# Routing keys fetched back from DRAM one batch at a time, and the last two slots' gating on VectorE

## The chip, the cores and the metric

The kernel runs on one core of a Trainium2 chip. The metric is the device time of one execution in microseconds. The engines are TensorE (PE; PEld is its loading of weights), VectorE (DVE), ScalarE (ACT), GpSimd (POOL) and SyncE (SP), which here only issues DMAs. All of them run their own instructions in program order, so an instruction that waits holds everything behind it on its engine.

## The reference

Three layers, each fed by the one before: an attention with a memory (batch 4, 8 heads, 576 positions, 64 wide), a mixture of 8 experts in which each expert takes exactly 288 of the 2304 tokens, and a dense layer with a gated activation.

```python
logits = x @ w_gate                       # 2304 tokens x 8 experts
order = np.argsort(-logits.flatten())
for idx in order:                         # greedy: best pair first
    tok, e = (int(idx) // E, int(idx) % E)
    if assigned[tok] >= 0 or counts[e] >= cap:   # cap = 288
        continue
    assigned[tok] = e
    counts[e] += 1
...
h = np.maximum(x[mask] @ w1[e], 0.0)      # 512 -> 1024, per expert
out[mask] = h @ w2[e]                     # 1024 -> 512
...
h = x @ w_in                              # 512 -> 2048, all tokens
g = h * np.clip(h + 3.0, 0.0, 6.0) / 6.0
return g @ w_out                          # 2048 -> 512
```

## The kernel before

After attention (the first 270 us or so) the function `experts` works through 8 slots, one expert's 288 tokens each. A slot has two stages. Stage 1 is the expert's layer: 8 chunks of 128 hidden units (`order` with kind 0). Stage 2 is the dense layer on the same tokens: 16 chunks (kind 1). A chunk is a first product `l1` into a PSUM tile h (L1240, L1241, L1243), its activation on other engines (`ev`, L1249 on), and two chunks later (`LAG`) a second product `l2` that adds into four PSUM tiles acc (`mm3`, L1136 to L1138). From slot 1 on every factor is split into a high and a low part in a reduced fp32 format, so each chunk costs 24 matmuls of 288 columns.

Stage 1's activation is two ScalarE operations for t and gh, and VectorE's gl = t − gh (L1254). Stage 2's is t and pc on ScalarE (L1258, L1259), a second pass for t (L1260), the product t * pc on GpSimd (L1261), gh on ScalarE (L1262) and gl = t − gh on GpSimd (L1263). At the end of stage 1 `y_in` empties acc into yh (ScalarE) and yl (VectorE, L1210), the input of stage 2; at the end of stage 2 `out_units` empties acc into yo (half of them on VectorE, L1178), which are transposed and scattered to the output rows.

Weights: stage 1's come in as raw and are split by ScalarE and GpSimd (L1127, L1128). Of stage 2's, the odd chunks stay in SBUF (WB), the even ones are fetched already split, 512 KB a time, by SP (w<-hl, L1124) when one of a few buffers comes free.

The greedy assignment is done by the class `Router`, in phases, one per expert. Each phase takes the best open expert of each token (`best`), puts the key of each (token, expert) pair on rows (`turn`), spreads them over 128 partitions, and searches for the threshold that leaves 288 (`search`: compare all 2304 keys at L715, count, refine; four steps on the high halves rHw, then on the low halves rLw). `ids_units` then counts positions (roc at L946, the counting matmuls rp at L702) and makes the row lists (ids, L959). Phases from 2 on spread the keys through DRAM: `by_dram` writes them to kd (64 rows, L761) and reads each half back with each expert's row repeated on 16 partitions, 128 x 2304 of 16 bits, 576 KB (L765). Attention ends with one such call too.

A phase runs while an earlier slot computes: it is a generator, and `step`, called twice per chunk, takes as many of its pieces as the numbers that it yields allow (BACK = 6 after rHw's issue, SLACK = 2.3 per search step; RATE per call of `step`). So the pieces land between the chunks in program order; the tile framework then orders the instructions of each engine by its own estimate of when they can start. In the profiled execution the slots lie at 468 to 555 us (slot 1), 555 to 644, 644 to 738 (slot 3), 738 to 837 (slot 4), 837 to 924, 924 to 1006 and 1006 to 1087 (slot 7). The searches run in slots up to 4; slots 5 to 7 have none, and slots 6 and 7 have no routing.

Of the kernel before, what the change touches and what calls it, by code (L numbers as in the profile page):

```python
# [9 lines left out]
F32 = mybir.dt.float32  # L10
# [4 lines left out]
AF = mybir.ActivationFunctionType  # L15
OP = mybir.AluOpType
# [10 lines left out]
BACK = 6  # L27
# [487 lines left out]
class Router:  # L515
# [233 lines left out]
    def by_dram(self, wait=False):  # L749


        nc, ps, E, B, S = self.nc, self.ps, self.E, self.B, self.S
        n = 2 * E * B
        ks = self.wk.tile([n, S], U16, name="ks", bufs=1)
        kd = self.dram.tile([2, E, B, S], U16, name="kd", bufs=2)
        for i in range(2):
            c = slice(i * S // 2, (i + 1) * S // 2)
            p = ps.tile([128, 512], F32, name="rw", tag=self.tags[0], bufs=self.tags[1])
            self.mm(p[:n, :S // 2], self.RB.rearrange("p d e b -> p (d e b)"), self.XT[:, c], start=True, stop=True)
            nc.scalar.activation(ks[:, c], p[:n, :S // 2], AF.Copy)  # L760
        nc.sync.dma_start(kd.rearrange("d e b s -> (d e b) s"), ks)  # L761

        def back(d, W):
            src = kd[d].rearrange("e b s -> e (b s)")
            nc.sync.dma_start(W.rearrange("p b s -> p (b s)"), bass.AP(  # L765
                tensor=src.tensor, offset=src.offset, ap=[[B * S, E], [0, 128 // E], [1, B * S]]))
        back(0, self.Hw)
        low = lambda: back(1, self.Lw)
        if wait:
            return low  # L770
        low()

    def early(self, ps, *tags):

# [38 lines left out]
    def phase(self, s):  # L813
# [6 lines left out]
        if s < E - 1:  # L820
            if s:
                with self.later(s):
                    self.best(slice(0, B))
                yield 1 if s == 1 else 3
            self.turn(s <= 1)
            yield 1
            if s == 0:
                self.last_batch()
            elif s < DIRECT:
                yield from self.direct()  # L830
            else:
                low = self.by_dram(True)
                yield BACK
            half = SHARE if s <= 1 else 0
            Hs = self.search(self.Hw, cap - half, self.rowH, 2 * half)
            next(Hs)
            yield next(Hs)
            if s >= DIRECT:
                low()
            for y in Hs:  # L840
                yield y
            Bv = self.found
            nc.vector.tensor_scalar(self.cmp, self.Hw, Bv, None, op0=OP.is_equal)
            yield 1
            nc.vector.tensor_tensor(self.Lw, self.Lw, self.cmp, op=OP.mult)
            Ls = self.search(self.Lw, self.rem, self.rowL, 2 * half)
            next(Ls)

            m = wk.tile([128, 4, 32], F32, name="m", bufs=1)
            c = self.rowH[:, :, :32]  # L850
            if half:
                nc.vector.tensor_scalar(m, c, float(half), None, op0=OP.add)
                c = m
            nc.vector.scalar_tensor_tensor(m, c, cap, c, op0=OP.is_lt, op1=OP.mult)
            nc.vector.tensor_tensor(m, m, self.own[:, None, :].to_broadcast([128, 4, 32]), op=OP.mult)
            cnt = wk.tile([128, 1], F32, name="cnt", bufs=2)
            nc.vector.tensor_reduce(cnt, m, axis=AX.XY, op=OP.max)
            nc.vector.tensor_scalar(self.rem, cnt, -1.0, cap - half, op0=OP.mult, op1=OP.add)
            rhs = wk.tile([128, 2, E], F32, name="rhs", bufs=1)
            nc.vector.tensor_scalar(rhs[:, 0, :], self.sel, Bv, None, op0=OP.mult)  # L860
            yield 2
            for y in Ls:
                yield y
            nc.vector.tensor_scalar(rhs[:, 1, :], self.sel, self.found, None, op0=OP.mult)
            yield 2
            if s == 0:
                yield None
            ps = self.ps
            p = ps.tile([128, 512], F32, name="rp", tag="r", bufs=2)
            self.mm(p[:, :2 * E], self.onef, rhs.rearrange("p a e -> p (a e)"), start=True, stop=True)  # L870
            hl = wk.tile([128, 2, E], I32, name="hl", bufs=1)
            nc.vector.tensor_scalar(hl[:, 0, :], p[:, :E], 128.0, None, op0=OP.max)
            nc.vector.tensor_copy(hl[:, 1, :], p[:, E:2 * E])
            k = wk.tile([128, E], I32, name="k", bufs=1)
            th = wk.tile([128, E], I32, name="th", bufs=1)
            nc.vector.scalar_tensor_tensor(k, hl[:, 0, :], 16, hl[:, 1, :], op0=OP.logical_shift_left,
                                           op1=OP.bitwise_or)
            nc.vector.tensor_scalar(th, k, 31, -1, op0=OP.arith_shift_right, op1=OP.bitwise_xor)
            nc.vector.scalar_tensor_tensor(th, th, -2 ** 31, k, op0=OP.bitwise_or, op1=OP.bitwise_xor)
            thf = th.bitcast(F32)  # L880
            top = wk.tile([128, 1], F32, name="top", bufs=1)
            u = wk.tile([128, E], F32, name="u", bufs=1)
            nc.vector.tensor_reduce(top, thf, axis=AX.X, op=OP.max)
            nc.vector.scalar_tensor_tensor(u, thf, top, self.w8, op0=OP.is_equal, op1=OP.mult)
            nc.vector.tensor_reduce(code, u, axis=AX.X, op=OP.max)
            oe = wk.tile([128, NJ], F32, name="oe", bufs=1)
            nc.vector.tensor_scalar(oe, m2, code, None, op0=OP.is_equal)
            nc.vector.scalar_tensor_tensor(GQ[:, 0, :], mx, top, oe, op0=OP.is_gt, op1=OP.mult)
            nc.vector.scalar_tensor_tensor(GQ[:, 1, :], mx, top, oe, op0=OP.is_equal, op1=OP.mult)
        else:  # L890
            nc.vector.tensor_copy(code, self.left)
            nc.vector.tensor_scalar(GQ[:, 0, :], dead, 0.0, None, op0=OP.is_equal)
            nc.vector.memset(GQ[:, 1, :], 0.0)
# [132 lines left out]
def experts(ctx, tc, rt, x_dram, cv, w1, w2, out, ident, cap, B, S):  # L1026
# [184 lines left out]
            y.append(hl)  # L1211
        return y

    def l1_whole(kind, f, x, w, prev=None):
        p = ps.tile([128, 512], F32, name="h", tag="h", bufs=2)[:, :cap]
        for k in range(KC):
            rt.behind = nc.tensor.matmul(p, w[:, k * 128:(k + 1) * 128], x[k], start=(k == 0), stop=(k == KC - 1))  # L1217
            if prev is not None:
                after(tc, rt.behind, prev)
                prev = None  # L1220

        def ev():
            g = whole("g", "g", LAG + 2)
            if kind == 0:
                nc.scalar.activation(g, p, AF.Relu)
            else:
                t = act.tile([128, cap], F32, name="t", tag="t", bufs=2)
                pc = act.tile([128, cap], F32, name="pc", tag="pc", bufs=2)
                nc.scalar.activation(t, p, AF.Relu, bias=rt.three)
                nc.scalar.activation(pc, p, AF.Copy, scale=1.0 / 6.0)  # L1230
                nc.vector.scalar_tensor_tensor(g, t, 6.0, pc, op0=OP.min, op1=OP.mult)
            return g
        return ev

    def l1(kind, f, x, w, prev=None):
        hi, lo = w
        p = ps.tile([128, 512], F32, name="h", tag="h", bufs=2)[:, :cap]
        wk = [[z[:, k * 128:(k + 1) * 128] for z in (hi, lo)] for k in range(KC)]
# [9 lines left out]
        def ev():  # L1248
            gh, gl = parts("g", "g", LAG + 2)  # L1249
            t = act.tile([128, cap], F32, name="t", tag="t", bufs=2)  # L1250
            if kind == 0:
                nc.scalar.activation(t, p, AF.Relu)
                nc.scalar.activation(gh, p, AF.Relu)  # L1253
                nc.vector.tensor_tensor(gl, t, gh.bitcast(F32), op=OP.subtract)  # L1254
            else:

                pc = act.tile([128, cap], F32, name="pc", tag="pc", bufs=2)
                nc.scalar.activation(t, p, AF.Relu, bias=rt.three, scale=-1.0)  # L1258
                nc.scalar.activation(pc, p, AF.Copy, scale=1.0 / 6.0)  # L1259
                nc.scalar.activation(t, t, AF.Relu, bias=rt.six, scale=-1.0)  # L1260
                nc.gpsimd.tensor_tensor(t, t, pc, op=OP.mult)  # L1261
                nc.scalar.activation(gh, t, AF.Copy)  # L1262
                nc.gpsimd.tensor_tensor(gl, t, gh.bitcast(F32), op=OP.subtract)  # L1263
            return gh, gl
        return ev

# [53 lines left out]
    for i, (s, kind, f) in enumerate(order):  # L1320
# [14 lines left out]
        ahead(i)  # L1335
        for u in range(min(2 if kind else 1, len(conv)) if i else 0):
            conv.pop(0)()
        e = (l1 if s else l1_whole)(kind, f, X[s, 1] if kind else XT[s], W.pop((i, 0)) if s else raws[i][0],
                                    rt.behind if kind and f == 1 else None)
        step()  # L1340
        if len(pend) == LAG:
# [88 lines left out]
```

## Time and profile before

| | us |
|---|---|
| runs of the kernel before: 1089.23, 1094.15, 1103.21; median | 1094.15 |
| the profiled execution | 1098.72 |
| its span, first to last instruction | 1096.9 |
| PE busy in it | 946.6 (86%) |
| DVE busy | 642.8 (59%) |
| POOL busy | 629.9 (57%) |
| ACT busy | 594.4 (54%) |

The mean granted TensorE clock of the span is 0.944, where 1 is full speed. TensorE is the busiest engine by far. Its busy share is a mean over attention and slots, so the section of rows below cuts the span by slot. A row of windows gives the bounds of a stretch, its length, then busy time and (instructions) of PE, PEld, DVE, ACT and POOL, the granted clock, the busy share of the DMA engines and GB/s; timelines list instructions with the wait ahead of each in brackets; the chain of waits goes back from what ended last.

### The profile page before, as it was taken

How to read it: one execution, taken by the hardware profiler on the slowest of the kernel's cores; microseconds unless marked ns; L12 is line 12 of the kernel's file. 1: busy time of each engine (PE TensorE's matmuls, PEld its weight loads, DVE VectorE, ACT ScalarE, POOL GpSimd, SP SyncE). 2: the span in 40 equal slices, each digit the busy share in tenths (PEclk: the TensorE clock that was granted, in tenths of full speed). 3: DMA queues.
4: the chain of work that ended last, by engine and by line, in shares of the span. 5: the costliest groups of instructions: out<-in, count | busy, mean ns of one | idle time of the engine just before them, and what ended most of it. 6: DMA issues, size and time to landing. Idle time of an engine off the chain costs nothing.

```text
span 1096.9 us, 19574 instructions
## 1 busy us (share of the span) xinstructions
PE 946.6 (86%) x6556; PEld 849.3 (77%) x6556; DVE 642.8 (59%) x1594; ACT 594.4 (54%) x1490; POOL 629.9 (57%) x595
## 2 busy tenths in 40 slices
PE   3898998998229897779999999899799999999996
PEld 3677776776127665569998998898798999999996
DVE  8689896876876878951962875845656400300300
ACT  5877776865315542434554564464355456456453
POOL 7665566560413573664674585476358558558553
PEclk9999999999559889899999999899899999999999
DMA  6887868785136566368437628724942842852540
GB/s 155 237 228 228 233 178 243 188 231 161 44 99 196 196 219 176 115 204 246 149 102 237 193 75 242 199 75 129 239 145 68 255 164 67 262 176 69 188 152 22
DMA packets 122707, 186.04 MB, mean 170 GB/s; under 512 B 21872, under 2 KB 72432, under 8 KB 122608
## 3 DMA queue, kind: packets, MB, share of 16 engines
q1 hardware_dynamic: 118848, 175.34, 53.8%
q0 software_dynamic: 3072, 9.44, 2.9%
q8 instruction: 52, 0.85, 0.3%
q14 instruction: 47, 0.39, 0.1%
q10 hardware_dynamic: 688, 0.02, 0.0%
HBM read 142.50 MB, written 23.51 MB: 151 GB/s over the span
## 4 chain that ended last, share of the span: by engine, by line
PE 48%; DVE 19%; DMA 12%; POOL 7%; issue 6%; ACT 5%; SPq 2%; POOLq 0%; ACTq 0%; DVEq 0%
PE h L1240 6%; PE h L1241 6%; PE h L1243 6%; PE acc L1137 6%; PE acc L1138 5%; PE acc L1136 5%; DVE rcmp L715 4%; DMA raw<-in_moe_w_in_dram 2%; POOL gl L1263 2%; PE av L328 2%; PE h L1217 2%; POOL t L1261 2%; DMA w<-hl 2%; DMA rHw<-kd 2%; PE acc L1270 2%
## 5 line engine op out<-in xcount | busy, mean ns | idle before, releaser
L1128 POOL TENSOR_TENSOR w<-raw,w 128x512 fp32r<-128x512 f32 x126 | 171.0, 1369 | 64.7 <-ACT w L1127 62.6
L1261 POOL TENSOR_TENSOR t<-t,pc 128x288 f32<-128x288 f32 x112 | 92.5, 828 | 95.2 <-ACT t L1260 95.2
L1254 DVE TENSOR_TENSOR gl<-t,gh 128x288 fp32r<-128x288 f32 x56 | 42.9, 772 | 173.1 <-ACT gh L1253 171.8
L1137 PE MATMUL acc<-gl,w 128*128 128x288 f32 x448 | 129.9, 302 | 16.3 <-POOL gl L1263 8.9
L1138 PE MATMUL acc<-gh,w 128*128 128x288 f32 x448 | 128.2, 298 | 0.0
L1136 PE MATMUL acc<-gh,w 128*128 128x288 f32 x448 | 109.0, 303 | 4.1 <-DVE yo L1178 2.6
L1258 ACT ACTIVATE t<-h,rthree 128x288 f32<-128x288 f32 x112 | 56.1, 501 | 101.4 <-PE h L1243 74.4
L1263 POOL TENSOR_TENSOR gl<-t,gh 128x288 fp32r<-128x288 f32 x112 | 90.9, 817 | 30.7 <-ACT gh L1262 30.7
L282 ACT ACTIVATE P<-P,mx 128x128 f32<-128x128 f32 (+2 forms) x144 | 83.7, 582 | 40.8 <-DVE mx L267 36.7
L1127 ACT ACTIVATE w<-raw 128x512 fp32r<-128x512 f32 x126 | 78.3, 632 | 43.4 <-PE acc L1138 21.3
L1137 PEld LDWEIGHTS acc<-gl,w 128*128 128x128 f32 x448 | 84.9, 190 | 20.7 <-POOL gl L1263 11.7
L1138 PEld LDWEIGHTS acc<-gh,w 128*128 128x128 f32 x448 | 85.2, 191 | 0.0
L1262 ACT ACTIVATE gh<-t 128x288 fp32r<-128x288 f32 x112 | 49.7, 444 | 59.4 <-POOL t L1261 59.1
L1136 PEld LDWEIGHTS acc<-gh,w 128*128 128x128 f32 x448 | 75.5, 190 | 5.7 <-DVE yo L1178 3.1
L246 PE MATMUL sc<-kh,qs 128*128 128x128 f32 (+3 forms) x128 | 49.8, 399 | 27.1 <-DVE mx L267 13.6
L1240 PE MATMUL h<-yh,w 128*128 128x288 f32 x224 | 64.2, 305 | 5.3 <-DMA w<-hl 3.5
L1074 POOL DMA_INDIRECT xg<-x_dram,ids x24 | 23.3, 970 | 78.6 <-DVE ids L959 28.8
L1240 PE MATMUL h<-xh,w 128*128 128x288 f32 x224 | 66.0, 313 | 1.9 <-ACT w L1127 1.9
L267 DVE CUSTOM_DVE_ANT_0 P<-sc,mask 128x128 f32<-128x128 f32 (+3 forms) x128 | 59.3, 480 | 11.2 <-PE sc L247 9.9
L1137 PE MATMUL acc<-gl,WB 128*128 128x288 f32 x224 | 64.4, 297 | 1.3 <-POOL gl L1263 1.3
L1241 PE MATMUL h<-xh,w 128*128 128x288 f32 x224 | 64.5, 307 | 0.1
L1138 PE MATMUL acc<-gh,WB 128*128 128x288 f32 x224 | 63.8, 295 | 0.0
(323 smaller groups left out, 2949.9 us busy)
## 6 DMA issues: line engine op xcount, KB each, us to landing
w<-hl SPq DMA_DIRECT2D x112, 512.0 KB, 4.9
raw<-in_moe_w_dram SPq DMA_DIRECT2D x128, 256.0 KB, 3.1
kh<-knh SPq DMA_DIRECT2D x60, 144.0 KB, 2.6
raw<-in_moe_w_in_dram SPq DMA_DIRECT2D x16, 512.0 KB, 4.6
raw<-in_moe_w_out_dram SPq DMA_DIRECT2D x16, 512.0 KB, 4.3
hl<-w SPq DMA_DIRECT2D x16, 512.0 KB, 2.9
wb<-wf SPq DMA_DIRECT2D x20, 256.0 KB, 4.4
raw<-wb SPq DMA_DIRECT2D x20, 256.0 KB, 2.7
```

The lines of the kernel that those rows point to most:

```text
L267: nc.vector.tensor_tensor_reduce(out=x[:, c0:c0 + cw], in0=sc[:, :cw], in1=m, scale=-scale, scalar=init, op0=OP.add, op1=OP.min, accum_out=mx)
L282: nc.scalar.activation(x[:, :w], x[:, :w], AF.Exp, bias=mx, scale=-1.0, accum_out=col)
L1127: nc.scalar.activation(hi, src, AF.Copy)
L1128: nc.gpsimd.tensor_tensor(lo, src, hi.bitcast(F32), op=OP.subtract)
L1136: nc.tensor.matmul(p, ah, bh, start=first, stop=False)
L1137: nc.tensor.matmul(p, ah, bl, start=False, stop=False)
L1138: rt.behind = nc.tensor.matmul(p, al, bh, start=False, stop=last)
L1240: nc.tensor.matmul(p, wk[k][0], x[k][0], start=(k == 0), stop=False)
L1241: nc.tensor.matmul(p, wk[k][1], x[k][0], start=False, stop=False)
L1243: rt.behind = nc.tensor.matmul(p, wk[k][0], x[k][1], start=False, stop=(k == KC - 1))
L1261: nc.gpsimd.tensor_tensor(t, t, pc, op=OP.mult)
L1263: nc.gpsimd.tensor_tensor(gl, t, gh.bitcast(F32), op=OP.subtract)
```

## The change

`by_dram` reads each half of the keys back in four pieces, one per batch of 576 tokens: 128 x 576, 144 KB, in rows of 1,152 bytes where before they had 4,608. Per phase, eight DMAs stand where two stood. `phase` issues the pieces of rHw one by one, with 0.8 between, and those of rLw one per search step; the numbers that it yields before the search sum to 6.4 (before: 6). The call in attention issues all eight in a row.

The activation of stage 2 in slots 6 and 7 drops the second pass of t on ScalarE. There t = relu(h + 3), and one VectorE scalar_tensor_tensor takes the minimum with 6 and multiplies by pc; gl = t − gh goes to VectorE too. GpSimd does nothing of the gating in these slots. Over 32 chunks that is 32 ScalarE and 64 GpSimd operations fewer and 64 VectorE operations more.

```diff
--- before.py
+++ after.py
@@ -760,15 +760,15 @@
             nc.scalar.activation(ks[:, c], p[:n, :S // 2], AF.Copy)
         nc.sync.dma_start(kd.rearrange("d e b s -> (d e b) s"), ks)
 
-        def back(d, W):
-            src = kd[d].rearrange("e b s -> e (b s)")
-            nc.sync.dma_start(W.rearrange("p b s -> p (b s)"), bass.AP(
-                tensor=src.tensor, offset=src.offset, ap=[[B * S, E], [0, 128 // E], [1, B * S]]))
-        back(0, self.Hw)
-        low = lambda: back(1, self.Lw)
+        def back(d, W, b):
+            src = kd[d, :, b]
+            nc.sync.dma_start(W[:, b], bass.AP(
+                tensor=src.tensor, offset=src.offset, ap=[[B * S, E], [0, 128 // E], [1, S]]))
+        pieces = [lambda d=d, W=W, b=b: back(d, W, b) for d, W in ((0, self.Hw), (1, self.Lw)) for b in range(B)]
         if wait:
-            return low
-        low()
+            return pieces
+        for u in pieces:
+            u()
 
     def early(self, ps, *tags):
 
@@ -829,15 +829,21 @@
             elif s < DIRECT:
                 yield from self.direct()
             else:
-                low = self.by_dram(True)
-                yield BACK
+                pieces = self.by_dram(True)
+                yield 1
+                for i in range(B):
+                    pieces[i]()
+                    yield 0.8 if i < B - 1 else BACK / 2
             half = SHARE if s <= 1 else 0
             Hs = self.search(self.Hw, cap - half, self.rowH, 2 * half)
             next(Hs)
             yield next(Hs)
             if s >= DIRECT:
-                low()
-            for y in Hs:
+                pieces[B]()
+            for i, y in enumerate(Hs):
+                if s >= DIRECT:
+                    for u in pieces[B + 1 + i:B + 2 + i]:
+                        u()
                 yield y
             Bv = self.found
             nc.vector.tensor_scalar(self.cmp, self.Hw, Bv, None, op0=OP.is_equal)
@@ -1211,7 +1217,7 @@
             y.append(hl)
         return y
 
-    def l1_whole(kind, f, x, w, prev=None):
+    def l1_whole(s, kind, f, x, w, prev=None):
         p = ps.tile([128, 512], F32, name="h", tag="h", bufs=2)[:, :cap]
         for k in range(KC):
             rt.behind = nc.tensor.matmul(p, w[:, k * 128:(k + 1) * 128], x[k], start=(k == 0), stop=(k == KC - 1))
@@ -1232,7 +1238,7 @@
             return g
         return ev
 
-    def l1(kind, f, x, w, prev=None):
+    def l1(s, kind, f, x, w, prev=None):
         hi, lo = w
         p = ps.tile([128, 512], F32, name="h", tag="h", bufs=2)[:, :cap]
         wk = [[z[:, k * 128:(k + 1) * 128] for z in (hi, lo)] for k in range(KC)]
@@ -1254,13 +1260,19 @@
                 nc.vector.tensor_tensor(gl, t, gh.bitcast(F32), op=OP.subtract)
             else:
 
+
                 pc = act.tile([128, cap], F32, name="pc", tag="pc", bufs=2)
-                nc.scalar.activation(t, p, AF.Relu, bias=rt.three, scale=-1.0)
-                nc.scalar.activation(pc, p, AF.Copy, scale=1.0 / 6.0)
-                nc.scalar.activation(t, t, AF.Relu, bias=rt.six, scale=-1.0)
-                nc.gpsimd.tensor_tensor(t, t, pc, op=OP.mult)
+                if s >= E - 2:
+                    nc.scalar.activation(t, p, AF.Relu, bias=rt.three)
+                    nc.scalar.activation(pc, p, AF.Copy, scale=1.0 / 6.0)
+                    nc.vector.scalar_tensor_tensor(t, t, 6.0, pc, op0=OP.min, op1=OP.mult)
+                else:
+                    nc.scalar.activation(t, p, AF.Relu, bias=rt.three, scale=-1.0)
+                    nc.scalar.activation(pc, p, AF.Copy, scale=1.0 / 6.0)
+                    nc.scalar.activation(t, t, AF.Relu, bias=rt.six, scale=-1.0)
+                    nc.gpsimd.tensor_tensor(t, t, pc, op=OP.mult)
                 nc.scalar.activation(gh, t, AF.Copy)
-                nc.gpsimd.tensor_tensor(gl, t, gh.bitcast(F32), op=OP.subtract)
+                (nc.vector if s >= E - 2 else nc.gpsimd).tensor_tensor(gl, t, gh.bitcast(F32), op=OP.subtract)
             return gh, gl
         return ev
 
@@ -1335,7 +1347,7 @@
         ahead(i)
         for u in range(min(2 if kind else 1, len(conv)) if i else 0):
             conv.pop(0)()
-        e = (l1 if s else l1_whole)(kind, f, X[s, 1] if kind else XT[s], W.pop((i, 0)) if s else raws[i][0],
+        e = (l1 if s else l1_whole)(s, kind, f, X[s, 1] if kind else XT[s], W.pop((i, 0)) if s else raws[i][0],
                                     rt.behind if kind and f == 1 else None)
         step()
         if len(pend) == LAG:
```

What the diff does not show is that the framework's order shifts with the new numbers. Three places follow, rows as they stand in the program of each engine.

VectorE at the turn from slot 3 to slot 4 (yo empties the sums of slot 3; roc and roh belong to the counting of the phase that runs here). Before:

```order
L940 SCALAR_TENSOR_TENSOR c<-ta,pos 128x20
L688 TENSOR_TENSOR rm_188<-rm_188,rdead 128x20
L946 TENSOR_TENSOR roc<-roc_4039,c 128x960 x2
L689 TENSOR_TENSOR roh<-rv,rm_188 128x160
L1254 TENSOR_TENSOR gl<-t,gh 128x288
L1178 COPY yo<-acc_8134 128x288
L695 TENSOR_TENSOR rX<-rB_175,roh 128x640
L1178 COPY yo<-acc_8136 128x288
```

After, the same place, with what now stands ahead of the chain:

```order
L687 TENSOR_REDUCE rm_188<-rv 128x20
L1260 TENSOR_TENSOR gl<-t,gh 128x288
L1184 COPY yo<-acc_8155 128x288
L1184 COPY yo<-acc_8157 128x288
L1260 TENSOR_TENSOR gl<-t,gh 128x288 x2
L914 TENSOR_SCALAR ex<-rp 128x2
L917 SCALAR_TENSOR_TENSOR pos<-sc,ex,GQ 128x20
```

Both yo have moved from behind roc and roh to ahead of the whole chain, whose roc stands 13 rows further on.

VectorE at the turn from stage 1 to stage 2 of slot 4 (L715 to L727 are the search on rHw, yl the input of stage 2). Before:

```order
L1254 TENSOR_TENSOR gl<-t,gh 128x288 x4
L715 TENSOR_SCALAR rcmp,cnt<-rHw,rT_137 128x2304
L724 STREAM_TRANSPOSE rrowH<-cnt 128x32
L727 SCALAR_TENSOR_TENSOR fl,T<-rrowH,rG 128x33
L715 TENSOR_SCALAR rcmp,cnt<-rHw,T 128x2304
L723 TENSOR_SCALAR rG<-T,rcz 128x1
L1210 TENSOR_TENSOR yl<-acc_8934,yh 128x288
L1210 TENSOR_TENSOR yl<-acc_8935,yh 128x288
```

After:

```order
L961 COPY rsv<-rp 96x6
L963 TENSOR_TENSOR d<-rsv 96x6
L1260 TENSOR_TENSOR gl<-t,gh 128x288 x2
L965 SCALAR_TENSOR_TENSOR ids<-d 96x3
L1260 TENSOR_TENSOR gl<-t,gh 128x288
L1216 TENSOR_TENSOR yl<-acc_8964,yh 128x288
L1216 TENSOR_TENSOR yl<-acc_8965,yh 128x288
L1216 TENSOR_TENSOR yl<-acc_8966,yh 128x288
L1216 TENSOR_TENSOR yl<-acc_8967,yh 128x288
L715 TENSOR_SCALAR rcmp,cnt<-rHw,rT_137 128x2304
```

The yl have moved ahead of the search, and ids ahead of them; in slots 2 and 3 the program before has yl ahead of the search as well.

SP in slot 3 (w_8085 before and w_8111 after are the same weights). Before:

```order
L1124 DMA w_7985<-hl 128x1024
L1124 DMA w_8058<-hl 128x1024
L761 DMA kd<-ks 64x576
L1124 DMA w_8060<-hl 128x1024
L1124 DMA w_8087<-hl 128x1024
L765 DMA rHw<-kd 128x1x2304
L1124 DMA w_8118<-hl 128x1024
L765 DMA rLw<-kd 128x1x2304
L1124 DMA w_8085<-hl 128x1024
L1124 DMA w_8167<-hl 128x1024
L1124 DMA w_8169<-hl 128x1024
```

After:

```order
L1130 DMA w_7999<-hl 128x1024
L1130 DMA w_8082<-hl 128x1024
L1130 DMA w_8084<-hl 128x1024
L761 DMA kd<-ks 64x576
L1130 DMA w_8113<-hl 128x1024
L1130 DMA w_8139<-hl 128x1024
L765 DMA rHw<-kd 128x1x576 x3
L1130 DMA w_8111<-hl 128x1024
L765 DMA rHw<-kd 128x1x576
L765 DMA rLw<-kd 128x1x576
L1130 DMA w_8186<-hl 128x1024
L765 DMA rLw<-kd 128x1x576 x3
```

That w has moved from behind rHw and rLw to ahead of the last piece of rHw and all of rLw. In slot 4 the order before is kd, w, raw, rHw, w, rLw, w, and after it is kd, two w, four pieces of rHw, two w, two of rLw, one w, two of rLw.

## Rows read from the trace of the kernel before

**Rows 1.** Windows of slots 3 to 7: us, busy (count), clock, DMA, GB/s

```profile
644.00:738.00 94.00, 86.21 (x636) 83.59 (x635) 58.92 (x118) 47.67 (x118) 57.22 (x59) 0.96 0.57 163
738.00:837.00 99.00, 88.26 (x639) 85.69 (x639) 58.31 (x122) 47.47 (x117) 56.07 (x58) 0.93 0.53 154
837.00:924.00 87.00, 82.81 (x645) 81.12 (x644) 21.80 (x39) 45.87 (x113) 57.46 (x58) 1.00 0.50 160
924.00:1006.00 82.00, 80.00 (x601) 78.93 (x601) 12.97 (x16) 45.69 (x113) 54.24 (x58) 1.00 0.52 169
1006.00:1087.00 81.00, 80.64 (x609) 80.25 (x608) 13.28 (x17) 42.05 (x103) 43.53 (x48) 1.00 0.35 119
```

**Rows 2.** Windows of the stretches around four stalls, and of an undisturbed one

```profile
695.00:704.00 9.00, 5.49 (x26) 5.29 (x25) 8.86 (x19) 1.67 (x4) 1.88 (x4) 0.65 0.72 215
745.00:753.00 8.00, 5.41 (x30) 5.13 (x30) 6.53 (x8) 2.30 (x7) 4.26 (x3) 0.79 0.31 98
776.00:790.00 14.00, 7.46 (x30) 6.71 (x30) 13.06 (x21) 3.33 (x8) 4.83 (x6) 0.63 0.97 235
996.00:1006.00 10.00, 8.37 (x59) 7.54 (x59) 0.00 (x0) 6.84 (x18) 8.60 (x10) 1.00 0.23 76
1050.00:1080.00 30.00, 30.00 (x227) 30.00 (x227) 0.00 (x0) 15.62 (x38) 15.26 (x19) 1.00 0.26 88
```

**Rows 3.** Waits of PE from 400 us on: instruction <- releaser: us, times, longest

```profile
PE acc L1137 <- DVE gl L1254: 7.4, 4, 3.1
PE h L1243 <- DVE yl L1210: 6.5, 1, 6.5
PE h L1240 <- DMA w<-hl: 3.5, 1, 3.5
PE rp L702 <- DVE roc L946: 2.9, 3, 1.5
PE acc L1136 <- DVE yo L1178: 2.6, 1, 2.6
```

**Rows 4.** Timeline of DVE in slot 4: start, us, instruction [idle before <- releaser]

```profile
748.17 0.45 DVE L1178 COPY yo<-acc 128x288 f32<-128x288 f32 x1
...
776.77 2.61 DVE L715 TENSOR_SCALAR_CACHE_REDUCE rcmp<-rHw,rT 128x2304 uint16<-128x2304 uint16 x1 [5.89 <-DMA rHw<-kd]
...
782.57 1.54 DVE L1210 TENSOR_TENSOR yl<-acc,yh 128x288 fp32r<-128x288 f32 x4
```

**Rows 5.** Timeline of DVE in slot 3, yl

```profile
678.93 1.55 DVE L1210 TENSOR_TENSOR yl<-acc,yh 128x288 fp32r<-128x288 f32 x4 [1.07 <-ACT yh L1209]
```

**Rows 6.** The chain of waits in slot 3: start, us, what

```profile
669.25 7.91 DMA out_dram<-ob,ids
...
681.50 0.41 PE h L1243 x3
...
681.93 17.18 DMA w<-hl
```

**Rows 7.** Timeline of SP in slot 3, the keys' issues

```profile
678.73 0.67 SPq L765 DMA_DIRECT2D rHw<-kd  x1
...
679.96 0.60 SPq L765 DMA_DIRECT2D rLw<-kd  x1
```

**Rows 8.** Windows: keys and weights in flight (slot 3), weights alone (slot 6)

```profile
680.00:700.00 20.00, 16.13 (x118) 15.69 (x117) 11.52 (x20) 9.57 (x24) 10.32 (x13) 0.94 0.98 213
945.00:955.00 10.00, 10.00 (x78) 10.00 (x77) 3.40 (x8) 2.74 (x8) 3.50 (x5) 1.00 0.93 323
```

**Rows 9.** Single lines: count, ns min/median/max, first and last start

```profile
L1231 DVE SCALAR_TENSOR_TENSOR g<-t,pc x16: 410/451/1554, 374.0 to 456.1; 128x288 f32<-128x288 f32 x16
L1254 DVE TENSOR_TENSOR gl<-t,gh x56: 424/459/3450, 466.1 to 1031.2; 128x288 fp32r<-128x288 f32 x56
L765 SPq DMA_DIRECT2D rHw<-kd x6: 653/678/718, 250.5 to 767.6; - x6
```

**Rows 10.** The page's part 6: DMA issues, KB each, us to landing

```profile
kh<-knh SPq DMA_DIRECT2D x60, 144.0 KB, 2.6
```

## The prediction

> **What bounds the kernel now.** I read the windows by slot first, then the list of waits of TensorE, then the timelines at the three worst places. A reader should look in [rows 1] at the length of a slot against its matmuls. Where nothing disturbs TensorE, 227 matmuls take 30.00 us [rows 2], so one takes 0.1322 us. The last slots, which carry no search, are close to that: slot 7 holds 609 matmuls in 81.00 us, 0.133 each. Slots 3 and 4 hold 636 and 639 and take 94.00 and 99.00 us, while slot 5 holds 645 and takes 87.00. So TensorE sets the time, and the 7 and 12 us that slots 3 and 4 have over slot 5 are stalls and their aftermath. The aftermath is visible in the granted clock: it is 1.00 in slots 5 to 7 and falls to 0.96 and 0.93 in slots 3 and 4, and to 0.63 and 0.65 in the stretches around the two longest stalls [rows 2]. I therefore price a stall by a stretch from its start until the clock is back: length less matmuls times 0.1322 us. A few per cent of the records can be missing, so such a price can be some tenths of a us high.
>
> Then the waits [rows 3] say which instruction was late: yl (6.5 us, once), w from DRAM (3.5, once), roc (2.9 in three), yo (2.6, once), and VectorE's gl (7.4 in four). Each of the first four sits beside the routing that runs in a slot for a later one.
>
> **Slot 4, yl.** In [rows 4] the search step at 776.77 is first kept 5.89 us by the return of the keys, then runs 2.61 us, and a second one follows before yl starts at 782.57. These four yl are what the next stage's first chunk multiplies, and TensorE stood still until 783.07. The new order of VectorE has yl ahead of the search, as slot 3 has it already: there yl started at 678.93, 1.07 us after it could [rows 5], and no wait for yl stands in the list of waits beside that of slot 4. The stretch from 776 to 790 is 14.00 us for 30 matmuls: 14.00 − 30 × 0.1322 = **−10.0 us**, if yl no longer waits for keys. This is the largest term, and it comes from the place of the search, not from how fast keys return.
>
> **Slot 4, yo.** Before, yo stands behind the whole chain of counting and starts at 748.17 [rows 4]; the first chunk of the new stage cannot write its sums until yo has emptied them. Now both yo stand ahead of the chain that ends in roc. The stretch from 745 to 753: 8.00 − 30 × 0.1322 = **−4.0 us**.
>
> **What slot 4 inherits.** The new order there is that of slot 3, with ids ahead of the last gl and of yl. In slot 3 ids waited for the scatter of rows from 669.25 to 677.17 [rows 6], and gl, which TensorE needed, stood behind it; the list of waits has 7.4 us for such gl in four times, the longest 3.1. I take +2.0; the ends are 0, if the scatter is over, and 3.1. The late weight of slot 3 (next) gets a counterpart too: in slot 4 one w now stands behind all of rHw and half of rLw, 864 KB, three quarters of what it stood behind in slot 3. I take +1.5, between 0 and the 5.6 that slot 3 shows. **+3.5 us**.
>
> **Slot 3, the late w.** TensorE waits 3.51 us for one w [rows 3]. Its DMA took 17.18 us from 681.93 [rows 6] because rHw and rLw had been issued at 678.73 and 679.96 and were ahead of it [rows 7]. In that stretch DMA was busy 0.98 of the time and moved 213 GB/s, whereas with weights alone it moved 323 at 0.93 [rows 8]: keys, which are read in rows and spread over 128 partitions, cost the queues more per byte. The new order puts this w ahead of the last quarter of rHw and of all rLw, 144 + 576 KB. By 213 GB/s these take 0.74 MB / 0.213 = 3.5 us, the whole wait; since keys are dearer than the mean of that stretch, rather more. The stretch from 695 to 704 lost 9.00 − 26 × 0.1322 = 5.6 us. **−5.5 us**; ends 0 (the w still late by as much as before) and −5.6.
>
> The w itself is issued when its buffer comes free (in the chain the last matmuls ahead of the issue end at 681.91 [rows 6]), and now the last piece of rHw and all of rLw wait on SP behind it. The search follows them by as much, and nothing of this slot waits for the search once yl is ahead of it.
>
> **Slot 2, roc.** Three waits of the counting matmuls for roc, 2.9 us together [rows 3]. The chain that makes roc now goes ahead of the yo in slot 2, so roc comes earlier and yo later. I take **−2.5 us**, between 0 (yo takes roc's place in the list of waits) and −2.9; the clock after these short waits I leave uncounted.
>
> **Slots 6 and 7, gating on VectorE.** Per chunk, ScalarE loses one activation and GpSimd two operations; VectorE gains two, which I price by the nearest rows, the same scalar_tensor_tensor of slot 0 (median 451 ns) and the gl of stage 1 (459) [rows 9]. That is 32 × 0.91 = 29 us of VectorE, which is idle for some 69 of 82 and 68 of 81 us in these slots [rows 1]. GpSimd, busy 54 of 82 us in slot 6, also splits the weights of slot 7 there. The stretch from 996 to 1006 lost 10.00 − 59 × 0.1322 = 2.2 us. In slot 7 nothing is lost (609 × 0.1322 = 80.5 of 81.0). So 32 chunks of shorter work buy **−2.0 us**, all of it in the tail of slot 6, with ends 0 and −2.2.
>
> The row of gl reaches 3450 ns and that of the scalar_tensor_tensor 1554 [rows 9], so one VectorE operation can be stretched several times over. The Trainium skill (SBUF — State Buffer, section Who interferes with whom) says that a VectorE instruction with two SBUF inputs contends with a GpSimd instruction that reads SBUF, and that the later one blocks until the first ends; both new operations are of that kind, and it speaks against this part of the change. These long maxima agree with it. In rows: a blocked pair costs up to 1.55 + 3.45 us, beside the 24 × 0.1322 = 3.2 us of a chunk and a lead of two chunks, so at worst the gain of 2.0 is lost.
>
> **Eight DMAs for two.** SP issues a return in 678 ns [rows 9]; six more per phase are 4.1 us of SP's time, 36 in all. Cover: w is issued chunks ahead, and weights are not late where keys are absent (the one such wait is in slot 3 [rows 3]). If the cover is gone, each phase's next w is up to 4.1 us later. Rows of 1,152 bytes instead of 4,608 were not run; the nearest is kh, also 144 KB a DMA, landing in 2.6 us [rows 10], which leaves nothing to add if pieces overlap, and at most 4 × 2.6 = 10.4 us for a set that lands one piece after the other. Nothing on TensorE's path waits for keys any more once yl is ahead. I take 0, with +4.1 in each of five slots as the other end.
>
> **The sum.** −10.0 − 4.0 + 3.5 − 5.5 − 2.5 − 2.0 = −20.5 us, against the profiled execution's 1098.7 (span 1096.9): 1078.2. The median of the runs shown is 1094.15, 4.6 lower, and their lowest is 1089.2; stalls of DMA may be shorter in those, and so would the gain be, so I don't take off all of the 4.6, but 1: **1077 us**, 1.6% under the median. This kernel's measurement tells about 2% from no change (1072.3 to 1116.0), so the forecast lies within it.
>
> **The rivals.**
> 1. The order gains, the weights don't. If slot 4 becomes a full copy of slot 3, a late w and its clock cost 5.6 rather than 1.5, the gl 3.1 rather than 2.0, and slot 3's w stays late because SP is held longer: 1077 + 4.1 + 1.1 + 5.5 = 1088. For it: the new order of slot 4 has a w behind six pieces. Against: in slot 3 it has five weights and three pieces ahead, less than before.
> 2. All goes well. With nothing inherited and slot 2's and 6's losses gone to their ends, the sum is −10.0 − 4.0 − 5.6 − 2.9 − 2.2 = −24.7, and with the full 4.6: 1069. For it: slots 3 and 4 would then take 94 − 5.6 = 88 and 99 − 14 = 85 us, about what slot 5 takes. Against: ids, which has to wait somewhere.
> 3. The other side: slower. Mechanism: the small pieces hold the one queue that also fetches w. Per phase 4.1 us more of SP's issue, and if 16 queues handle 4 times the rows no faster per byte, every phase gets a w late by as much as slot 3's, at 5.6 us with its clock. Five phases: 28 us, on top of the yl gain: 1077 + 5.5 (slot 3 not mended) + 28 = 1110, slower than now. It decides from some 3.5 us of added lateness per slot on. For it: 0.98 of DMA at 213 GB/s says that keys are paid by row and not by byte. Against: the queues' wait for rHw no longer holds TensorE. The Trainium skill (DMA: Bandwidth & Descriptors, section on bandwidth) gives 64 KB as the size under which descriptors dominate and asks for 1 MiB; 144 KB lies between, and no run here shows the split.
> 4. Gating on VectorE gains nothing, for the blocking above: 1079. It is inside the forecast.
>
> **How the numbers follow.** Forecast, with rival 4 in it, 1073 to 1083: 0.45. Rival 1, 1083 to 1094: 0.18. Rival 2, 1061 to 1073: 0.29. Rival 3: 0.08. The range 1064 to 1090 leaves out the lowest quarter of rival 2, a third of rival 1 and rival 3, some 0.2. Under 1072.3 lies most of rival 2: 0.28. Over 1116 the worst of rival 3: 0.05. Rest: 0.67.
>
> **What would show it.** In the windows, slot 4 at 86 to 89 us with its clock near 0.99 shows both order terms; slot 3 at 88 to 89, and w absent from the waits, shows the split; slots 6 and 7 at 80 and 81 the gating. A wait of TensorE for gl behind ids in slot 4 is what is inherited. The prediction is wrong if yl still stands after a wait for keys, if w appears in the waits of three slots or more, or if a wait for gl on VectorE shows up in slots 6 and 7.

## The result, and the profile after

The changed kernel takes 1082.95 us in the median (1078.09 to 1085.68) against 1095.71 for the kernel before: ratio 0.987, 95% interval 0.9829 to 0.991, so 10 to 19 us are gained. That is faster by more than the noise, by less than 2%, and inside the range of 1064 to 1090; of the forecast 18.7 us (1095.7 − 1077) some 13 came. The profiled execution is the longest of the four, 1085.68 us, its span 1083.9.

The windows by slot come first (bounds, length, busy time and count of PE, PEld, DVE, ACT and POOL, granted clock, DMA share, GB/s), for slots 2 to 7 (3 to 7 as in [rows 1]), and then one stretch in which slot 3 lost time:

```profile
558.50:648.00 89.50, 83.31 (x637) 81.12 (x635) 58.06 (x111) 47.29 (x116) 56.77 (x59) 1.00 0.53 170
648.00:740.00 92.00, 85.74 (x635) 83.36 (x634) 62.43 (x127) 47.79 (x118) 56.45 (x59) 0.96 0.55 167
740.00:826.50 86.50, 83.25 (x635) 81.22 (x635) 56.11 (x107) 47.17 (x117) 58.29 (x58) 1.00 0.57 176
826.50:913.50 87.00, 82.61 (x648) 81.21 (x647) 21.27 (x45) 46.17 (x113) 55.20 (x58) 1.00 0.50 160
913.50:993.00 79.50, 79.14 (x602) 78.88 (x601) 28.88 (x47) 39.16 (x97) 31.55 (x28) 1.00 0.53 170
993.00:1074.00 81.00, 80.64 (x610) 80.33 (x609) 29.91 (x50) 35.36 (x87) 16.55 (x14) 1.00 0.37 123
...
725.00:736.00 11.00, 7.57 (x41) 7.09 (x40) 9.49 (x30) 4.23 (x12) 5.98 (x7) 0.69 0.10 32
```

Slot 4 went from 99.0 to 86.5 us, its clock from 0.93 to 1.00; slot 6 from 82.0 to 79.5; slots 5 and 7 are as long as before. Slot 3 fell only from 94 to 92, since the stretch from 725 to 736 is new. The waits of TensorE from 400 us on (us in total, times, longest), as in [rows 3]:

```profile
...
PE acc L1143 <- DVE gl L1260: 8.5, 4, 3.6
PE acc L1143 <- POOL gl L1275: 7.2, 9, 1.3
PE acc L1142 <- DVE yo L1184: 3.9, 2, 2.4
PE rp L702 <- DVE rhs L870: 2.1, 1, 2.1
PE rp L702 <- DVE roc L952: 2.1, 2, 1.6
...
PE rp L702 <- DVE ob L1196: 1.2, 1, 1.2
```

The waits for yl and for w are gone. In their place: yo waits in two other places (at the turns of slots 1 and 4), roc in slot 3 instead of slot 2, and two that were not there, for rhs and for ob. VectorE at the end of stage 1 of slot 4, against [rows 4]:

```profile
771.55 0.16 DVE L965 SCALAR_TENSOR_TENSOR ids<-d 96x3 int32<-96x3 f32 x1 [6.62 <-DMA out_dram<-ob,ids]
771.66 0.46 DVE L1260 TENSOR_TENSOR gl<-t,gh 128x288 fp32r<-128x288 f32 x1
773.19 1.55 DVE L1216 TENSOR_TENSOR yl<-acc,yh 128x288 fp32r<-128x288 f32 x4 [1.07 <-ACT yh L1215]
```

yl now waits for nothing but yh, and gl stands behind an ids that waited 6.62 us for the scatter, as forecast; TensorE lost 1.24 us there.

### The profile page after: what moved, and what is told of

The parts are those of the page before. It is cut to its first block, busy times and chain, and to the rows that moved or that the text cites. A ratio compares the mean times of both kernels' runs of the same rounds, so it can differ in the third digit from the quotient of the medians.

```text
span 1083.9 us, 19609 instructions
## 1 busy us (share of the span) xinstructions
PE 944.3 (87%) x6555; PEld 847.8 (78%) x6556; DVE 684.2 (63%) x1658; ACT 581.4 (54%) x1458; POOL 577.7 (53%) x531
## 4 chain that ended last, share of the span: by engine, by line
PE 50%; DVE 21%; issue 10%; DMA 8%; POOL 4%; ACT 4%; SPq 2%; POOLq 0%; DVEq 0%; ACTq 0%
PE h L1246 6%; PE h L1247 6%; PE acc L1143 5%; PE h L1249 5%; PE acc L1144 5%; DVE rcmp L715 5%; PE acc L1142 5%; PE av L328 3%; PE h L1223 2%; PE tp L313 2%; PE acc L1282 1%; PE sc L246 1%; PE mem L374 1%; DVE roc L952 1%; DMA rHw<-kd 1%
## 5 line engine op out<-in xcount | busy, mean ns | idle before, releaser
L1144 PE MATMUL acc<-gh,w 128*128 128x288 f32 x448 | 127.6, 296 | 0.0
L1142 PE MATMUL acc<-gh,w 128*128 128x288 f32 x448 | 112.4, 302 | 5.4 <-DVE yo L1184 3.9
L1260 DVE TENSOR_TENSOR gl<-t,gh 128x288 fp32r<-128x288 f32 x56 | 48.6, 874 | 104.1 <-ACT gh L1259 103.8
L1273 POOL TENSOR_TENSOR t<-t,pc 128x288 f32<-128x288 f32 x80 | 65.4, 819 | 56.3 <-ACT t L1272 56.3
L1275 POOL TENSOR_TENSOR gl<-t,gh 128x288 fp32r<-128x288 f32 x80 | 66.1, 831 | 19.6 <-ACT gh L1274 19.6
L1270 ACT ACTIVATE t<-h,rthree 128x288 f32<-128x288 f32 x80 | 40.1, 501 | 67.5 <-PE h L1249 45.6
L1199 POOL DMA_INDIRECT out_dram<-ob,ids x24 | 25.4, 1059 | 87.8 <-ACT ob L1198 74.6
L1246 PE MATMUL h<-xh,w 128*128 128x288 f32 x224 | 65.0, 309 | 0.4 <-ACT w L1133 0.4
L1258 ACT ACTIVATE t<-h 128x288 f32<-128x288 f32 x56 | 23.0, 411 | 76.7 <-PE h L1249 72.4
```

Source lines behind the costliest of these rows:

```text
L1142: nc.tensor.matmul(p, ah, bh, start=first, stop=False)
L1144: rt.behind = nc.tensor.matmul(p, al, bh, start=False, stop=last)
L1246: nc.tensor.matmul(p, wk[k][0], x[k][0], start=(k == 0), stop=False)
L1275: (nc.vector if s >= E - 2 else nc.gpsimd).tensor_tensor(gl, t, gh.bitcast(F32), op=OP.subtract)
```

## The experiments

Two explanations stood against each other. A: the gain is the new order of VectorE (yl and yo ahead), as the prediction had it. B: it is the small pieces, whatever the order. The first four runs take the change apart on one chip, beside the same runs of the kernel before (1097.54 us).

**The yielded number alone.**

```diff
-BACK = 6
+BACK = 6.4
```

> The kernel before with one number changed: 6.4 instead of 6 is yielded ahead of the search. Keys return in one piece per half and GpSimd does all the gating. The order of VectorE becomes that of the changed kernel in slots 1, 3 and 4 (yl ahead of the search, yo ahead of the counting chain). Theory A (the order of VectorE carries the gain): 1084 to 1089 us against about 1095, no wait for yl in slot 4, and one or two waits for w of 3 to 4 us, since both halves of the keys are still ahead of a w. Theory B (the small pieces carry the gain): 1092 us or more.

1093.43 us in the median of ten (1086.67 to 1101.26), ratio 0.9975 (0.9945 to 1.0005). The profile is of the shortest of them. Its waits of TensorE from 470 us on:

```profile
PE acc L1137 <- DVE gl L1254: 11.9, 5, 4.2
...
PE h L1240 <- DMA w<-hl: 4.4, 2, 2.6
PE acc L1136 <- DVE yo L1178: 3.9, 2, 2.4
```

The wait for yl is gone, w is late twice, as A had expected. The time is not A's: about 4 us of gain in the median, with an interval that reaches past zero.

**Pieces, in the order of before.**

```diff
-                low = self.by_dram(True)
+                pieces = self.by_dram(True)
+                for u in pieces[:B]:
+                    u()
                 yield BACK
```

> The keys return in four pieces per half, but the pieces of a half are issued together and the numbers yielded are those of the kernel before, so that slot 4 keeps two search steps ahead of yl. No change of the gating. Theory A: the wait for yl in slot 4 stays, at 4 to 7 us; only what the pieces do for w is gained, 1089 to 1094 us. Theory B: most of the gain is here, 1083 to 1087 us.

1084.29 us (1082.55 to 1085.74), ratio 0.9881 (0.9838 to 0.9925). Its waits of TensorE:

```profile
PE acc L1140 <- POOL gl L1266: 10.1, 13, 1.3
PE acc L1140 <- DVE gl L1257: 7.2, 4, 3.0
PE h L1246 <- DVE yl L1213: 5.4, 1, 5.4
PE rp L702 <- DVE roc L949: 2.9, 3, 1.5
PE acc L1139 <- DVE yo L1181: 2.7, 1, 2.7
```

yl, roc and yo wait as in the kernel before, w never does, and nearly the whole gain is there. That is B. What A had forecast for this run, 1089 to 1094, did not come.

**The whole change of the keys, without the gating.** (The diff above, of `by_dram` and `phase`, alone.)

> The whole change of the keys' return (pieces and yielded numbers), without the change of the gating. Theory A: 1084 to 1087 us, 2 to 3 more than the changed kernel (1083), and 1 to 4 less than with the yielded number alone, because w no longer stands behind all keys. If the pieces cost queue time that weights need, it is slower than with the yielded number alone.

1083.25 us (1081.82 to 1084.74), ratio 0.9871 (0.9828 to 0.9915). So by the medians of these runs the order is worth about 4 us with whole halves (1097.5 to 1093.4) and about 1 with pieces (1084.3 to 1083.3); the pieces are worth 13 in the old order and 10 in the new one.

**The gating alone.** (The diff above, of `l1`, alone.)

> Only the gating of slots 6 and 7 on VectorE; keys return as before. Theory A: 2 to 3 us less than before (1092 to 1093), all of it from the last chunks of slot 6, and slot 7 as long as before. Rival (VectorE is blocked by GpSimd there): 1095, with waits of TensorE for VectorE's gl in slots 6 and 7.

1093.22 us (1087.89 to 1100.03), ratio 0.9964 (0.9927 to 1.0001): 4 us, not apart from zero.

**Why pieces help.** In the return of before, the 16 partitions of one expert are filled from the same 4,608 bytes of DRAM. The next run returns the keys by the same two DMAs per phase and in rows as long, but no bytes are read twice (the rows of ks are put in another order for it, which is not shown):

```diff
-        kd = self.dram.tile([2, E, B, S], U16, name="kd", bufs=2)
+        R = 128 // E
+        kd = self.dram.tile([2, E, R, B, S], U16, name="kd", bufs=2)
...
-        nc.sync.dma_start(kd.rearrange("d e b s -> (d e b) s"), ks)
+        for b in range(B):
+            m = 2 * E
+            nc.sync.dma_start(kd[:, :, :, b].rearrange("d e r s -> (d e) r s"),
+                              ks[m * b:m * (b + 1), None, :].to_broadcast([m, R, S]))
...
+            nc.sync.dma_start(W.rearrange("p b s -> p (b s)"), kd[d].rearrange("e r b s -> (e r) (b s)"))
```

> The kernel before, but the keys are written to DRAM 16 times (four broadcast writes of 295 KB more per phase instead of one of 72 KB), so that in the return, still one DMA per half in rows of 4,608 bytes, no two partitions read the same bytes. In the traces so far a row of 4,608 bytes takes 346 ns in the median and one of 1,152 bytes 51 ns. Theory C (16 partitions reading the same DRAM row at once slow each other and the weights beside them): rows of 4,608 bytes fall to 180 to 230 ns, weights in the stretch of the return to under 250 ns from 290 to 350. Theory D (long rows are what is slow): they stay at 320 ns or more. The time is for the writes' sake no clean measure: 1088 to 1098 us by C, 1097 to 1105 by D.

**Rows half as long.** (Two pieces per half, issued together, in the order of before; the issuing is not shown.)

```diff
+            nc.sync.dma_start(W[:, b:b + 2].rearrange("p b s -> p (b s)"), bass.AP(
+                tensor=src.tensor, offset=src.offset, ap=[[B * S, E], [0, 128 // E], [1, 2 * S]]))
```

> Two pieces of two batches per half, rows of 2,304 bytes, issued together, gating as before. If the gain goes with the length of the row: rows of 2,304 bytes take 110 to 170 ns and the time lies between, 1086 to 1092 us. If it only takes that a half is not one DMA: about 1084, as with four pieces.

Beside 1098.64 us for the kernel before, the copies take 1089.15, ratio 0.9931 (0.9906 to 0.9957), though they write 1.1 MB more per phase; the halves 1092.62, ratio 0.9945 (0.9923 to 0.9967), just above the 1086 to 1092 that had been expected. The copies' time is no clean measure: their order moved too, so that in slot 4 yl (at 767.18) stands ahead of the search (at 780.33) and TensorE no longer waits for it, while w is still late twice, by 1.7 and 1.4 us. The better evidence is in the DMA packets of the traces, one row of a return each. Worked out from all packets of the five returns after 400 us, without the writing of kd; the last column has the 4,096-byte rows of the weights that started during a return, the lowest and the highest median of the five:

```
kernel              bytes  read by        median ns  ns per KB  DMA time, us  weights' rows, ns
before               4608  16 partitions       359         80           461         159 to 352
before, once more    4608  16 partitions       359         80           461         159 to 341
copies               4608  one                 178         40           264         159 to 188
halves               2304  16 partitions       131         58           362         159 to 282
quarters (e2)        1152  16 partitions        51         45           320         159 to 202
```

The length of the row alone isn't what is slow: unshared, 4,608 bytes take 178 ns. With 16 partitions to one row they take twice that, and in four of the five returns the weights' rows beside them take 268 to 352 ns in the median instead of 159. With rows of 1,152 bytes, shared as well, a KB costs 45 ns, and the weights take at most 202 (241 in the changed kernel): much less, though not nothing.

That it is the sharing is likely and not shown, because the copies change one thing more. In the kernel before, with halves and with quarters, mostly eight rows of a return are in flight at a time and hardly ever more than nine; with the copies ten or more are for half of the time. Eight at a time alone doesn't make a row slow, since it holds for the quarters too, but long unshared rows, eight at a time, were not run.

The windows of the return in slot 3 show the same in bulk, of the kernel before, of the copies (a wider stretch around it) and of the changed kernel:

```profile
690.80:707.80 17.00, 13.49 (x85) 13.29 (x84) 16.61 (x36) 6.04 (x15) 5.16 (x7) 0.80 0.79 209
```

```profile
690.00:710.00 20.00, 20.00 (x153) 20.00 (x152) 17.61 (x29) 10.55 (x26) 10.62 (x13) 1.00 0.72 254
```

```profile
693.30:713.20 19.90, 19.90 (x152) 19.90 (x152) 15.31 (x28) 9.94 (x25) 10.66 (x14) 1.00 0.80 249
```

At a like busy share the DMA engines move 209, 254 and 249 GB/s, and TensorE is whole in the last two.

**The kernel before, once more.**

> The kernel before once more, for a second profile of it. Executions of it lie between 1089 and 1107 us, those of the kernels with small pieces between 1078 and 1086. If late weights are what varies, this profile has waits of TensorE for w in other places or sizes (one of 3.5 us in the first), and the waits that hang on the order of VectorE (yl 6.5, yo 2.6, roc 2.9) within 1 us of the first.

1096.55 us. Its waits of TensorE:

```profile
PE h L1243 <- DVE yl L1210: 7.1, 1, 7.1
...
PE h L1240 <- ACT w L1127: 3.0, 1, 3.0
PE rp L702 <- DVE roc L946: 2.9, 3, 1.5
PE acc L1136 <- DVE yo L1178: 2.6, 1, 2.6
...
PE h L1240 <- DMA w<-hl: 1.0, 1, 1.0
```

What hangs on the order repeats ([rows 3]: 6.5, 2.9, 2.6); the wait for w is 1.0 instead of 3.5, and the longest for a weight being split 3.0 instead of 1.9. So the waits on weights are what differs most between these two executions. That they also make the longer executions of the yielded number alone isn't shown: its profile is of the shortest.

**The gating, sized on one chip.** The changed kernel again, and the same without the gating:

> The changed kernel once more, beside the next one on the same chip, to size the gating of slots 6 and 7 alone. If the gating is worth what the profiles show in the tail of slot 6 (2.2 to 2.8 us), it is 2 to 3 us below the next one; if VectorE's operations there are blocked by GpSimd, the two are equal within 1 us.

> The changed kernel without the change of the gating, as before: about 1083 to 1085 us; against the changed kernel see there.

1081.31 us (1076.67 to 1088.62), ratio 0.9852 (0.9819 to 0.9885), and 1081.85 (1080.37 to 1082.24), ratio 0.986 (0.9839 to 0.9881). By these medians the gating is worth nothing that can be seen. The profiles can be cut where the medians can't: by the start of the first yl of slots 1 and 5 in VectorE's timelines, in us.

| profile of | to slot 1's yl | to slot 5's yl | to the end |
|---|---|---|---|
| before; once more | 502.3; 503.6 | 368.5; 364.9 | 226.2; 226.3 |
| yielded number alone | 501.9 | 356.3 | 226.7 |
| pieces, order of before | 496.3 | 359.7 | 226.2 |
| pieces, new order; again | 498.1; 498.1 | 356.9; 353.4 | 226.7; 227.1 |
| gating alone | 499.5 | 367.4 | 223.5 |
| changed kernel; again | 506.3; 505.0 | 353.6; 352.0 | 224.0; 224.4 |

The last column is the gating: 226.2 to 227.1 without it, 223.5 to 224.4 with it, some 2.6 us in these profiles. The middle one is the keys: 367 in the mean before, 354 with pieces in the new order. The first one varies by 10 us, although the changed kernel and the one without the gating have the same instructions on every engine up to slot 6. There the two profiles of the changed kernel lost 7 to 8 us. That the same hides the gating in the medians is likely and not shown; what makes that stretch long or short is open.

The table also sets a limit to what the medians said of pieces and order. Pieces in the order of before took 7 us off the middle stretch, most of it between slot 3's yl and slot 4's (103.6 us in the first profile of the kernel before, 96.5 with pieces), where w had been late. The rest of their 13 us lies in the first stretch, and how they would gain it there isn't shown. The order is worth 11 us of the middle stretch by itself (356.3 against 367, in the shortest of its runs) and 3 to 8 on top of the pieces (359.7 against 352.0 to 356.9), more than the 4 and 1 of the medians. What the order is worth is open within these bounds. That the pieces give nearly the whole gain without it is not.

VectorE's price of the gating, minimum, median and maximum in ns of the changed kernel:

```profile
L1268 DVE SCALAR_TENSOR_TENSOR t<-t,pc x32: 457/459/510, 946.3 to 1070.1; 128x288 f32<-128x288 f32 x32
...
L1275 DVE TENSOR_TENSOR gl<-t,gh x32: 451/459/1215, 947.3 to 1071.1; 128x288 fp32r<-128x288 f32 x32
```

**Can the order's gain be kept?** In the changed kernel ids waits for the scatter that still reads an old list; with four lists instead of two it need not:

```diff
-            ids = wk.tile([96, 3], I32, name="ids", bufs=2)
+            ids = wk.tile([96, 3], I32, name="ids", bufs=4)
```

> The changed kernel with four buffers for ids instead of two. In the trace of the changed kernel ids waits 19.3 us in five times for the scatter that still reads the old lists, VectorE stands still with it, and gl for TensorE behind it (8.5 us in four waits). If that is what took back the gain of the order, these waits go and the time falls by 4 to 8 us, to 1075 to 1079. If the waits of gl have another cause, no change (within 2 us).

1083.17 us (1077.97 to 1088.64), ratio 0.988 (0.9856 to 0.9904): no change, where 1075 to 1079 had been expected. TensorE's waits for VectorE's gl fell from 8.5 us in four to 5.4 in two, and its middle stretch is 350.7 us, but the last one is 228.1 for 224.0, and GpSimd's gl is late there (3.8 us in that stretch, 1.5 in the changed kernel):

```profile
PE acc L1143 <- POOL gl L1275: 9.8, 10, 2.5
PE acc L1143 <- DVE gl L1260: 5.4, 2, 3.4
```

**More gating on VectorE, on top of it.**

```diff
-                if s >= E - 2:
+                if s >= E - 3 or f >= FB - 4:
```

> The one before, with the gating on VectorE in slot 5 too, and in the last four chunks of every slot from 1 on. In the changed kernel TensorE loses 2.0 to 2.2 us to GpSimd's gl at the end of each of slots 1 to 5; with 2 of them gone per slot: 8 to 10 us below the one before, if VectorE has the time there beside the search (it is busy 60% of slots 2 to 4); 2 to 4 us slower than it if the gating is held up by the search.

1095.9 us, ratio 0.9995 (0.9971 to 1.0019): 13 us slower than with four lists alone, which is worse than both outcomes that had been expected. Its waits of TensorE:

```profile
PE xt L1161 <- ACT xh L1173: 20.2, 4, 8.5
PE acc L1143 <- DVE gl L1260: 8.2, 4, 5.2
```

In the tails of slots 1 to 4 the gating takes its place on VectorE behind the search. ScalarE's gh needs VectorE's t, and xh, which makes the next slot's input, stands behind gh on ScalarE. ScalarE's timeline at the end of slot 1:

```profile
547.10 0.44 ACT L1274 ACTIVATE gh<-t 128x288 fp32r<-128x288 f32 x1 [8.15 <-DVE t L1268]
547.45 0.61 ACT L1133 ACTIVATE w<-raw 128x512 fp32r<-128x512 f32 x1
548.07 0.41 ACT L1172 ACTIVATE t<-xt 128x288 f32<-128x288 f32 x1
548.38 0.40 ACT L1173 ACTIVATE xh<-xt 128x288 fp32r<-128x288 f32 x1
```

So xh comes late, and TensorE waits for it in four slots.

**Without the tails.**

```diff
-                if s >= E - 3 or f >= FB - 4:
+                if s >= E - 3:
```

> The changed kernel with four buffers for ids, and the gating on VectorE in slot 5 too, but not in the tails of slots 1 to 4, where the kernel before this one had TensorE wait up to 8.5 us for ScalarE's xh. In the profile with four buffers, GpSimd's gl costs 1.6 and 4.8 us of TensorE at the end of slot 5 and the start of slot 6; with these gone and nothing new: 1076 to 1080 us, the fastest so far. If the clock or another wait gives it back, 1081 to 1085 as the others.

1075.49 us (1071.28 to 1081.85), ratio 0.9822 (0.9784 to 0.986). It is the fastest measured, 20 us under the kernel before. Against the changed kernel (0.9852, 0.9819 to 0.9885, on another chip) the intervals overlap, so the 3 us between them are likely and not shown.

## Why the prediction was right, and where its steps failed

The time fell inside the range and on the side that was forecast, but most of the gain has another reason than the one given for it.

- **Eight DMAs for two, taken at 0.** This is the step that failed. It bounded the pieces from nothing up to a loss, and left out a gain. In either order they are worth 10 to 13 us by the medians, most of the result. The row to see it by was there: 213 against 323 GB/s at a like busy share [rows 8]. The prediction read it as "read in rows and spread over 128 partitions", a property of keys; the pieces show that shorter rows relieve it, and the copies, with more rows in flight at a time, that keys in unshared rows cost no more per byte than weights do (40 ns per KB each). The Trainium skill (DMA: Bandwidth & Descriptors, section Bandwidth) would batch DMAs to 1 MiB or more; here four of 144 KB were faster than one of 576 KB.
- **Slot 4, yl and yo, −14.0.** The mechanism was right in its place: both waits went, and slot 4 lost 12.5 us with its clock back at 1.00, at the edge of the forecast 86 to 89. But "the largest term … comes from the place of the search" isn't borne out over the whole kernel: by the medians the order is worth about 4 us without the pieces and 1 with them, by the middle stretch of the profiles 11 and 3 to 8. It is one order for all slots, and it opened other waits: yo at the turns of slots 1 and 4 (3.9 us), ob, and the next point.
- **"Nothing of this slot waits for the search."** This failed in slot 3. The chain of waits of the changed kernel there:

```profile
726.04 2.62 DVE rcmp L715 x2
...
729.75 1.17 DVE rhs L870
...
730.96 0.61 PE rp L702 x2
731.58 0.43 PE h L1246
732.00 0.24 PE h L1247
```

  The search ran to the end of the slot, TensorE stood 2.1 us before the counting matmul that needs its result, and came back at the lower clock (0.24 us a matmul; 0.69 in the stretch). Slot 3 so took 92 us, where 88 to 89 had been said. The second profile of the changed kernel has no such loss.
- **Slot 3, the late w, −5.5.** Right as to the wait: no kernel with pieces of a quarter has one for w. The reason was only half the place behind the keys: with pieces in the order of before it is gone too.
- **Slot 2, roc, −2.5.** Nothing came of it: slot 2 took 89.0 us before and takes 89.5. The wait moved to slot 3, and yo and ob took its place, the lower end of that term.
- **What slot 4 inherits, +3.5.** gl behind ids cost 1.24 us of TensorE for 2.0; the late w, +1.5, did not come.
- **Gating, −2.0.** Right in size and place: 2.6 us in the last stretch of the profiles, slot 6 shorter by 2.5, slot 7 as long as before. The prices were right as well, 459 and 459 ns for 451 and 459. Rival 4, the blocking by GpSimd, did not decide: the longest gl took 1215 ns, and TensorE did not wait for VectorE's gating. Whether that one was held up by the rule of the Trainium skill (SBUF — State Buffer, section Who interferes with whom), no run here shows.
- **Rival 3, slower for the pieces.** It fell: six more issues a phase at 584 ns hid behind the cover that was named, and the rows got cheaper, not dearer.
- **The range.** That it held was luck in good part: the terms of the order came to 14.5 us, for 1 to 4 by the medians, and those of the pieces to 4.0, for 10 to 13, so that two errors of opposite sign made up for each other.

## What to carry to other kernels

When a broadcast from DRAM gives many partitions the same row, look at how long its packets take against rows of like length that nobody shares, and try shorter rows or copies if they are dear: here they slowed the weights in flight beside them. Price an order as a whole, since an instruction put ahead moves something else behind; here stalls that went in two slots came back as smaller ones in others. Where a part of the program that the change doesn't touch varies by more than the gain, compare stretches of the profiles and not only medians.

## What was not expected of the hardware

A row of 4,608 bytes takes 178 ns in the median if it fills one partition and 359 if it is read for 16; rows of 2,304 and 1,152 bytes read for 16 take 131 and 51. The weights' rows of 4,096 bytes, 159 ns with no return in flight, take up to 352 in the median of a return of the first kind of shared rows, and 188 at most beside the unshared ones. While seven to nine rows of a return are in flight, a weight's row takes 334 ns in the kernel before, 291 with halves, 252 with quarters and 159 with the copies.
